# A cross network's first layer: weights in three transfers, first products by input tile

## The chip, the cores and the metric

The kernel runs on one core of one Trainium2 chip. The metric is the device time of one execution in microseconds (us), of which the median over several runs is taken. A core has TensorE (PE in the profile, with PEld for its weight loads), VectorE (DVE), ScalarE (ACT), GpSimd (POOL), SyncE (SP, which issues nearly all DMAs here) and 16 DMA engines.

## The reference

Six layers of a cross network over 16384 rows of 416 features, in bfloat16:

```python
B, F, D, L = 16384, 26, 16, 6
Din = min(F * D, 1024)                      # 416
def reference(x0, ws, bs):
    x = x0
    for l in range(L):
        proj = jnp.einsum('bd,de->be', x, ws[l]) + bs[l]
        x = x0 * proj + x
    return x
```

## The kernel before

The rows are cut into 8 groups of 2048 (`GC`), a group into 4 chunks of 512 (`CH`, index `j`). On the chip x stands transposed: features on the partitions, rows along the free axis. The 416 features are three tiles of 128 (`NT` = 3, index `t` as input, `i` as output) and a tail of 32. A product is one matmul of a 128 x 128 piece of `wm[l]` with a 128 x 512 chunk of x into one of 8 PSUM banks; three products and a tail matmul (`w3[l]`, `rows32`) make one output tile of one chunk. `evacuate` then adds the bias on ScalarE, and multiplies by x0 and adds x on VectorE.

All instructions are put in order by hand: `add` appends each to the queue of its engine with the tokens it reads and writes, and `Program` works out the semaphore waits between engines. Within an engine the order is that of the calls. A token for PSUM is a whole bank, `("ps", b)`: a reader of a bank waits for the last writer of it that stands ahead of it, and a writer for all its earlier readers.

Groups other than the first are loaded by transposing DMAs. Group 0 is loaded in natural order, as rows on partitions, in eight transfers of half a chunk each (`load_nat(j, k0, k1)`, L758), and transposed on TensorE: `transposed_chunk(j)` (L813) makes 12 transposes of 128 x 128 for a chunk, six for its first half and six for its second, then copies the three tiles out of PSUM into `x0s`, on VectorE (L823) or on ScalarE (L825). Where the tiles of chunk j lie in PSUM is fixed by two banks:

```python
ba, bb = ((0, 1), (3, 0), (6, 7), (0, 1))[j]
place = ((ba, 0), (bb, 0), (ba, CH)) if j == 0 else ((ba, 0), (ba, CH), (bb, 0))
```

and a tile is copied by VectorE where `(b == bb) != (j == 1)`. So VectorE copies tile 1 of chunk 0, tiles 0 and 1 of chunk 1 and tile 2 of chunks 2 and 3, and ScalarE the others: two of chunk 0, one of chunk 1, two of chunk 2, two of chunk 3.

`first_job` is the start of the kernel: the transposes of chunk 0, those of the bias, fill matmuls on constants (`keep_busy(n, b)`, n pieces of 128 columns, L795), the products of chunk 0 for output tiles 0 and 1 (`full`, L668), the transposes of chunks 1 and 2, the products of chunk 1, the transposes of chunk 3 and the tails (`transposed_tails`, L833), and then the products of chunks 2 and 3 with their tail matmuls (L689), output tile by output tile. The products of chunk j go to banks `ba[j]` and `bb[j]` with `ba, bb = [4, 5, 6, 7], [2, 3, 0, 1]`.

Layer 0's weights are loaded in two transfers (`load_wm(0, "sp", f0, f1)`, L392): columns 0 to 255 (output tiles 0 and 1) behind chunk 0's rows, the others behind the tail weights (`load_w3`, L401). Then `load_group(1)` issues the transposing DMAs of group 1 (L411, L421). After the first job come two tiles of group 1 (`two_tiles`) and, for nearly all of the time, a stream of matmuls on 32-row strips whose order is a string in the code (`ORDER`, L1108 and L1112).

Of the kernel before, what the change touches and what calls it, by code (L numbers as in the profile page):

```python
# [3 lines left out]
P = 128  # L4
# [302 lines left out]
def bass_standalone__cross_network_dcn__recsys_kernel(  # L307
# [6 lines left out]
    B, D = x0.shape  # L314
# [61 lines left out]
    def bank(b, p0=0, p1=P, n=CH):  # L376
        return psum[p0:p1, b * CH:b * CH + n]
# [7 lines left out]

    W0 = 2 * P

    def load_wm(l, eng, f0=0, f1=D):  # L390
        toks = {0: [("wm", l)], W0: [("wm", l, "rest")]}[f0] if l == 0 else [("wm", l), ("wm", l, "rest")]
        add(eng, lambda h: h.dma_start(  # L392
            wm[l][:, :, f0:f1], ws[l, 0:NT * P, f0:f1].rearrange("(t p) f -> p t f", p=P)),
            writes=toks, lane=f"wm{l}_{f0}", batch=0)

    def wm_tok(l, i):
        return ("wm", l) if i < 2 else ("wm", l, "rest")

    def load_w3(l, eng):
        for j in range(NJ):  # L400
# [252 lines left out]
    def full(g, l, i, banks, first, chunk_major, after_chunk=None, chunks=range(NJ), ts_=range(NT), columns=False):  # L653
        src, stok = x_src(g, l)
        ecols = slice(i * P, (i + 1) * P)
        seq = [(t, j) for j in chunks for t in ts_] if chunk_major else \
              [(t, j) for t in ts_ for j in chunks]
        for t, j in seq:
            if columns:
                for c in range(NJ):  # L660
                    o = slice(c * T32, (c + 1) * T32)
                    add("pe", lambda h, t=t, j=j, c=c, o=o: h.matmul(  # L662
                        psum[o, banks[j] * CH:(banks[j] + 1) * CH],
                        wm[l][:, t, i * P + c * T32:i * P + (c + 1) * T32], src(t, j, j + 1),
                        start=(first and t == 0), stop=(not first and t == NT - 1), tile_position=(0, c * T32)),
                        reads=[stok(t, j), wm_tok(l, i)], writes=[("ps", banks[j])])
                continue
            add("pe", lambda h, t=t, j=j: h.matmul(  # L668
                bank(banks[j]), wm[l][:, t, ecols], src(t, j, j + 1),
                start=(first and t == 0), stop=(not first and t == NT - 1)),  # L670
                reads=[stok(t, j), wm_tok(l, i)], writes=[("ps", banks[j])])
            if after_chunk and t == NT - 1:
                after_chunk(j)

# [20 lines left out]
    def tails(batch, corners_last=False, banks=None):  # L695
# [14 lines left out]
        for (g, l), b in zip(batch, bs_):  # L710
            src, stok = x_src(g, l)
            for t in range(NT):
                for j in range(NJ):
                    ro, qo = quad(g, l + 1, j)
                    add("pe", lambda h, t=t, j=j, src=src, l=l, b=b, ro=ro, qo=qo: h.matmul(  # L715
                        psum[qo, b * CH:(b + 1) * CH], wm[l][:, t, NT * P:D], src(t, j, j + 1),
                        start=(corners_last and t == 0), stop=(not corners_last and t == NT - 1),
                        tile_position=(0, ro * T32)),
                        reads=[stok(t, j), wm_tok(l, NT)], writes=[("ps", b)])
            if not corners_last:  # L720
                evacuate_tail(g, l, b)
        if corners_last:
# [41 lines left out]
        reads=["warm"], writes=["warm"])  # L764
    load_nat(0, 0, 2)
    load_nat(0, 2, KK)
    load_wm(0, "sp", 0, W0)
    for j in range(1, NJ):
        load_nat(j, 0, 2)
        load_nat(j, 2, KK)  # L770
    load_w3(0, "sp")
    load_wm(0, "sp", W0, D)
    load_group(1)

    def second_tails():
# [51 lines left out]
    def transposed_tails(b):  # L827

        s = slot(0)
        for k in range(KK):  # L830
# [6 lines left out]
        add("dve", lambda h: h.tensor_copy(x0s[s][:, XW:XW + CH], psum_t(b)[:, 0:CH]),  # L837
            reads=[("ps", b)], writes=x03_toks(s))

    def first_job():  # L840

        g, l = 0, 0
# [7 lines left out]
        for j in range(NJ):  # L850
# [17 lines left out]
        transposed_tails(7)  # L868
        full(g, l, 0, ba, True, True, chunks=[2, 3])
# [194 lines left out]
    def stream(run):  # L1064
# [23 lines left out]
        for _, r, c, b in plan:  # L1088
# [18 lines left out]
            if t < NT:  # L1107
                add("pe", lambda h, l=l, t=t, j=j, b=b, q=q, ecols=ecols, src=src, kw=kw: h.matmul(  # L1108
                    bank(b), wm[l][q, t, ecols], src(t, j, j + 1)[q, :], **kw),
                    reads=[stok(t, j), wm_tok(l, i)], writes=[("ps", b)], row=r)  # L1110
# [60 lines left out]
    def nat_full(kk, j, b, first, ts=range(NT)):  # L1171
        for t in ts:
            add("pe", lambda h, t=t: h.matmul(  # L1173
                bank(b, n=D), xcol(t, j, kk), wm[l][:, t, :], start=(first and t == 0),
                stop=(not first and t == NT - 1)),
                reads=[stok(t, j), ("wm", l)], writes=[("ps", b)])

    def turn_last(j, b):

# [139 lines left out]
```

## Time and profile before

| | |
|---|---|
| median of 3 runs | 465.24 us (465.17 to 465.78) |
| the profiled execution | 465.03 us |
| its span, from the first to the last instruction | 463.2 us |
| TensorE busy | 458.1 us, 99% of the span |
| VectorE, ScalarE busy | 402.9 us, 87%; 382.2 us, 83% |
| fill matmuls before the first products | 4.90 to 5.35 us |
| first products (L668) start | 5.55 us |
| first tail matmul (L689) of the first output tile | 12.21 us |

The view by line gives busy time and the wait ahead of a group; the timeline gives start and length of each piece of work, merged where instructions of one kind follow each other, with the idle time ahead of it and what ended it in brackets. In the chain the times of a matmul are those of its end as modelled, some 0.15 us later than the starts in the timeline; times in the text are starts by the timeline. A start is counted from the span's start.

### The profile page before, as it was taken

The numbers are of one execution on the slowest core, as the hardware profiler recorded it, in microseconds if no ns is written. First come the engines' busy times: TensorE is split into PE (matmuls) and PEld (weight loads), VectorE is DVE, ScalarE is ACT, GpSimd is POOL, SyncE is SP. The second block draws the span as 40 slices with busy tenths as digits, with TensorE's granted clock in tenths as the row PEclk, the third lists the DMA queues.
The fourth block names the chain that finished last, engine by engine and source line by source line (L and its number), as shares of the span: only waits on it lengthen the run. The fifth ranks groups of instructions, "written<-read, shape, count | busy, mean of one in ns | idle before, by whom it ended". The sixth has DMA issues, their size and how long they took to land.

```text
span 463.2 us, 17830 instructions
## 1 busy us (share of the span) xinstructions
PE 458.1 (99%) x8001; PEld 266.1 (57%) x8001; DVE 402.9 (87%) x697; ACT 382.2 (83%) x609; POOL 10.7 (2%) x15
## 2 busy tenths in 40 slices
PE   9999999999999999999999999999999999999996
PEld 5444656575655556555665556566556565555552
DVE  2897898988889898898989889898988988989997
ACT  4686889887988889797888889888888888888785
POOL 1000000000000000000000000000000040000000
PEclk9999999999999999999999999999999999999999
DMA  8986759000002859086477965690000088171899
GB/s 229 188 178 148 153 110 195 14 23 10 17 4 37 145 178 192 15 131 182 89 130 137 196 104 94 104 226 17 25 2 4 25 143 299 41 132 43 213 163 307
DMA packets 136768, 53.78 MB, mean 116 GB/s; under 512 B 113258, under 2 KB 135284, under 8 KB 136692
## 3 DMA queue, kind: packets, MB, share of 16 engines
q1 hardware_dynamic: 136536, 52.54, 53.2%
q8 instruction: 62, 1.02, 0.9%
q10 hardware_dynamic: 156, 0.11, 0.1%
q14 instruction: 14, 0.11, 0.1%
HBM read 5.97 MB, written 13.63 MB: 42 GB/s over the span
## 4 chain that ended last, share of the span: by engine, by line
PE 94%; DVE 4%; DMA 1%; issue 0%; SPq 0%; ACT 0%; DVEq 0%
PE ps L1108 73%; PE ps L715 7%; PE ps L1112 6%; PE ps L668 4%; PE ps L662 1%; PE ps L703 1%; DVE x L1234 1%; DVE x L591 1%; DVE x L1228 1%; DMA wm<-in_ws_dram 1%; DVE tw L586 1%; PE ps L689 1%; PE ps L813 0%; SPq L758 0%; ACT tw L574 0%
## 5 line engine op out<-in xcount | busy, mean ns | idle before, releaser
L1108 PE MATMUL ps<-x,wm 32*128 32x512 bf16 x6288 | 372.8, 374 | 0.0
L574 ACT ACTIVATE tw<-ps,bias 128x512 bf16<-128x512 f32 x524 | 327.2, 688 | 48.5 <-PE ps L1108 35.8
L1108 PEld LDWEIGHTS ps<-x,wm 32*128 32x128 bf16 x6288 | 221.9, 92 | 135.5 <-ACT tw L574 6.5
L586 DVE TENSOR_TENSOR tw<-tw,x 128x1024 bf16<-128x1024 bf16 x262 | 177.2, 690 | 41.5 <-ACT tw L574 40.1
L591 DVE TENSOR_TENSOR x<-tw,x 128x1024 bf16<-128x1024 bf16 x262 | 170.5, 686 | 0.3
L1112 PE MATMUL ps<-x,w 32*128 32x512 bf16 x524 | 159.5, 374 | 0.0
L1112 PEld LDWEIGHTS ps<-x,w 32*128 32x128 bf16 x524 | 44.6, 92 | 6.0
L715 PE MATMUL ps<-x,wm 128*32 128x512 bf16 x564 | 33.6, 380 | 0.0
L635 ACT ACTIVATE ts<-ps,bias 128x512 bf16<-128x512 f32 x32 | 20.4, 686 | 13.1 <-PE ps L703 13.1
L538 ACT ACTIVATE tw<-ps,bias 128x1024 bf16<-128x1024 f32 (+1 forms) x24 | 20.7, 938 | 8.1 <-PE ps L689 7.0
L715 PEld LDWEIGHTS ps<-x,wm 128*32 128x32 bf16 x564 | 13.5, 96 | 18.2 <-ACT tw L574 3.7
L668 PE MATMUL ps<-x,wm 128*128 128x512 bf16 x92 | 21.3, 380 | 0.2 <-DMA wm<-in_ws_dram 0.2
L639 DVE TENSOR_TENSOR x<-ts,x 128x512 bf16<-128x512 bf16 x47 | 18.4, 420 | 0.3
L951 POOL COPY ost<-ot 128x512 bf16<-128x512 bf16 x6 | 9.2, 1534 | 389.8 <-DMA ot<-x 389.8
L547 DVE TENSOR_TENSOR tw<-tw,x 128x1024 bf16<-128x1024 bf16 (+1 forms) x21 | 13.1, 637 | 2.2 <-ACT tw L538 2.1
L668 PEld LDWEIGHTS ps<-x,wm 128*128 128x128 bf16 x92 | 8.4, 98 | 11.4 <-issue 2.1
L631 DVE SCALAR_TENSOR_TENSOR ts<-ps,bias,x 128x512 bf16<-128x512 f32 x15 | 11.2, 747 | 3.1 <-PE ps L703 3.1
L552 DVE TENSOR_TENSOR x<-tw,x 128x1024 bf16<-128x1024 bf16 (+1 forms) x21 | 12.6, 634 | 0.0
L637 DVE TENSOR_TENSOR ts<-ts,x 128x512 bf16<-128x512 bf16 x32 | 12.4, 418 | 0.0
L1173 PE MATMUL ps<-wm,x 128*128 128x416 bf16 x48 | 9.3, 340 | 0.0
L823 DVE COPY x<-ps 128x512 bf16<-128x512 bf16 x5 | 2.0, 423 | 8.1 <-PE ps L813 8.1
L1222 ACT ACTIVATE x<-ps 128x416 bf16<-128x416 f32 x16 | 7.7, 528 | 1.5 <-PE ps L1173 1.5
(51 smaller groups left out, 72.0 us busy)
## 6 DMA issues: line engine op xcount, KB each, us to landing
out_dram<-ost SPq DMA_DIRECT2D x6, 1664.0 KB, 8.3
x<-x SPq DMA_DIRECT2D x24, 96.0 KB, 2.2
x<-in_x_dram SPq DMA_DIRECT2D x8, 208.0 KB, 3.6
x<-in_x_dram SPq DMA_DIRECT2D x4, 416.0 KB, 8.0
wm<-in_ws_dram SPq DMA_DIRECT2D x5, 312.0 KB, 3.5
x<-x SPq DMA_DIRECT2D x22, 64.0 KB, 2.4
out_dram<-x SPq DMA_DIRECT2D x3, 416.0 KB, 3.2
out_dram<-ost SPq DMA_DIRECT2D x2, 416.0 KB, 3.1
```

What stands on the lines that cost most here:

```text
L538: add("act", lambda h, a=a, w=w, b0=b0: h.activation(tw[r][:, a * CH:(a + w) * CH], psum[:, b0 * CH:(b0 + w) * CH], ACT_F.Identity, bias=b ...
L547: add("dve", lambda h, a=a, e=e: h.tensor_tensor(tw[r][:, a * CH:e * CH], tw[r][:, a * CH:e * CH], x0s[s0][:, i * GC + a * CH:i * GC + e * ...
L552: add("dve", lambda h, a=a, e=e: h.tensor_tensor(xs[so][:, i * GC + a * CH:i * GC + e * CH], tw[r][:, a * CH:e * CH], src(i, a, e), ALU.ad ...
L574: add("act", lambda h: h.activation(tw[r][:, j * CH:(j + 1) * CH], bank(b), ACT_F.Identity, bias=bias[:, i, l:l + 1], scale=1.0), reads=[( ...
L586: add("dve", lambda h: h.tensor_tensor(tw[r][:, o], tw[r][:, o], x0s[s0][:, c], ALU.mult), reads=[("tw", r, k) for k in both] + [x0_tok(s0 ...
L591: add("dve", lambda h: h.tensor_tensor(xs[so][:, c], tw[r][:, o], src(i, a, a + 2), ALU.add), reads=[("tw", r, k) for k in both] + [stok(i ...
L635: add("act", lambda h: h.activation(ts[r][:, :], bank(b), ACT_F.Identity, bias=bias[:, 3, l:l + 1], scale=1.0), reads=[("ps", b), "bias"], ...
L639: add("dve", lambda h: h.tensor_tensor(x3s[so][:, :], ts[r][:, :], res, ALU.add), reads=[("ts", r)] + rtok, writes=[("x3", so), ("x3", so, ...
L668: add("pe", lambda h, t=t, j=j: h.matmul(bank(banks[j]), wm[l][:, t, ecols], src(t, j, j + 1), start=(first and t == 0), stop=(not first a ...
L715: add("pe", lambda h, t=t, j=j, src=src, l=l, b=b, ro=ro, qo=qo: h.matmul(psum[qo, b * CH:(b + 1) * CH], wm[l][:, t, NT * P:D], src(t, j, ...
L1108: add("pe", lambda h, l=l, t=t, j=j, b=b, q=q, ecols=ecols, src=src, kw=kw: h.matmul(bank(b), wm[l][q, t, ecols], src(t, j, j + 1)[q, :], ...
L1112: add("pe", lambda h, l=l, b=b, q=q, ecols=ecols, s3=s3, kw=kw: h.matmul(bank(b), w3[l][q, ecols], s3[q, :], **kw), reads=tok3 + [("w3", l ...
```

## The change

The first layer's weights come in three transfers of 104 KB, one for each input tile, all columns of it, in the order 1, 0, 2; there is no second transfer behind the tail weights. Each product of layer 0 waits for its own input tile only. The products of chunks 0 and 1 go by input tile: for each input tile both output tiles, in the order 1, 0, 2 for chunk 0 and 0, 2, 1 for chunk 1 (`by_copy`). The transposes of each half chunk follow the same order (1, 0, 2 for chunks 0, 2 and 3). `transposed_chunk` may make one half only: chunk 2's first half stands ahead of chunk 1's products, its second half with its copies behind them. The fill matmuls ahead of the first products shrink from 5 pieces of 128 columns to 2.

```diff
-    W0 = 2 * P
-    def load_wm(l, eng, f0=0, f1=D):
-        toks = {0: [("wm", l)], W0: [("wm", l, "rest")]}[f0] if l == 0 else [("wm", l), ("wm", l, "rest")]
+    def load_wm(l, eng):
         add(eng, lambda h: h.dma_start(
-            wm[l][:, :, f0:f1], ws[l, 0:NT * P, f0:f1].rearrange("(t p) f -> p t f", p=P)),
-            writes=toks, lane=f"wm{l}_{f0}", batch=0)
+            wm[l][:, :, :], ws[l, 0:NT * P, :].rearrange("(t p) f -> p t f", p=P)),
+            writes=[("wm", l, t) for t in range(NT)], lane=f"wm{l}", batch=0)
+    def load_wm_tile(l, t):
+        add("sp", lambda h: h.dma_start(wm[l][:, t, :], ws[l, t * P:(t + 1) * P, :]),
+            writes=[("wm", l, t)], lane=f"wm{l}_{t}", batch=0)
...
     load_nat(0, 0, 2)
     load_nat(0, 2, KK)
-    load_wm(0, "sp", 0, W0)
+    for t in (1, 0, 2):
+        load_wm_tile(0, t)
     for j in range(1, NJ):
         load_nat(j, 0, 2)
         load_nat(j, 2, KK)
     load_w3(0, "sp")
-    load_wm(0, "sp", W0, D)
     load_group(1)
...
-    def transposed_chunk(j):
+    def transposed_chunk(j, halves=(0, 2)):
...
-        for k2 in (0, 2):
-            for t in range(NT):
+        for k2 in halves:
+            for t in by_copy(j):
...
+        if 2 not in halves:
+            return
         for t in range(NT):
             b, o = place[t]
...
+    def by_copy(j):
+        return (0, 2, 1) if j == 1 else (1, 0, 2)
+
+    def by_input_tile(j, *bks):
+        src, stok = x_src(0, 0)
+        for n, t in enumerate(by_copy(j)):
+            for i, b in enumerate(bks):
+                add("pe", lambda h, n=n, t=t, i=i, b=b: h.matmul(
+                    bank(b[j]), wm[0][:, t, i * P:(i + 1) * P], src(t, j, j + 1),
+                    start=n == 0, stop=False), reads=[stok(t, j), ("wm", 0, t)], writes=[("ps", b[j])])
...
-        keep_busy(5, 3)
+        keep_busy(2, 3)
         ba, bb = [4, 5, 6, 7], [2, 3, 0, 1]
-        full(g, l, 0, ba, True, True, chunks=[0])
-        full(g, l, 1, bb, True, True, chunks=[0])
+        by_input_tile(0, ba, bb)
         transposed_chunk(1)
-        transposed_chunk(2)
-        full(g, l, 0, ba, True, True, chunks=[1])
-        full(g, l, 1, bb, True, True, chunks=[1])
+        transposed_chunk(2, (0,))
+        by_input_tile(1, ba, bb)
+        transposed_chunk(2, (2,))
         transposed_chunk(3)
         transposed_tails(7)
```

In the other places of the diff a product's token of the weights becomes `("wm", l, t)`.

More of the change, by code (lines that the diff above doesn't have):

```diff
@@ L384, in take @@
         return got
-    W0 = 2 * P
-    def load_wm(l, eng, f0=0, f1=D):
-        toks = {0: [("wm", l)], W0: [("wm", l, "rest")]}[f0] if l == 0 else [("wm", l), ("wm", l, "rest")]
+    def load_wm(l, eng):
         add(eng, lambda h: h.dma_start(
-            wm[l][:, :, f0:f1], ws[l, 0:NT * P, f0:f1].rearrange("(t p) f -> p t f", p=P)),
-            writes=toks, lane=f"wm{l}_{f0}", batch=0)
-    def wm_tok(l, i):
-        return ("wm", l) if i < 2 else ("wm", l, "rest")
+            wm[l][:, :, :], ws[l, 0:NT * P, :].rearrange("(t p) f -> p t f", p=P)),
[3 more added lines that the diff above has]
+            writes=[("wm", l, t)], lane=f"wm{l}_{t}", batch=0)
     def load_w3(l, eng):
@@ L665, in full @@
                         start=(first and t == 0), stop=(not first and t == NT - 1), tile_position=(0, c * T32)),
-                        reads=[stok(t, j), wm_tok(l, i)], writes=[("ps", banks[j])])
+                        reads=[stok(t, j), ("wm", l, t)], writes=[("ps", banks[j])])
                 continue
@@ L670, in full @@
                 start=(first and t == 0), stop=(not first and t == NT - 1)),
-                reads=[stok(t, j), wm_tok(l, i)], writes=[("ps", banks[j])])
+                reads=[stok(t, j), ("wm", l, t)], writes=[("ps", banks[j])])
             if after_chunk and t == NT - 1:
@@ L718, in tails @@
                         tile_position=(0, ro * T32)),
-                        reads=[stok(t, j), wm_tok(l, NT)], writes=[("ps", b)])
+                        reads=[stok(t, j), ("wm", l, t)], writes=[("ps", b)])
             if not corners_last:
@@ L1109, in stream @@
                     bank(b), wm[l][q, t, ecols], src(t, j, j + 1)[q, :], **kw),
-                    reads=[stok(t, j), wm_tok(l, i)], writes=[("ps", b)], row=r)
+                    reads=[stok(t, j), ("wm", l, t)], writes=[("ps", b)], row=r)
             else:
@@ L1175, in nat_full @@
                 stop=(not first and t == NT - 1)),
-                reads=[stok(t, j), ("wm", l)], writes=[("ps", b)])
+                reads=[stok(t, j), ("wm", l, t)], writes=[("ps", b)])
     def turn_last(j, b):
```

## The prediction

> **What bounds the kernel now.** I read the page first: TensorE (PE) is 99% busy, and the chain that ended last lies on it.
>
> ```profile
> PE 94%; DVE 4%; DMA 1%; issue 0%; SPq 0%; ACT 0%; DVEq 0%
> ```
>
> So a shift of TensorE's stream in the first 12 us, which is all that this change touches, reaches the end one for one: no later row shows a wait that could swallow it or add to it. Next the chain in order of time over the first 24 us (start, length, what):
>
> ```profile
> 1.65 3.76 DMA wm<-in_ws_dram
> 5.42 0.14 issue
> 5.55 1.46 PE ps L668 x6
> 7.00 1.00 PE ps L813 x18
> 8.01 0.03 issue
> 8.04 0.51 PE ps L813 x6
> 8.55 1.29 PE ps L668 x6
> 9.84 0.67 PE ps L813 x12
> 10.51 0.34 PE ps L833 x16
> 10.85 1.43 PE ps L668 x6
> ```
>
> The first products (L668) wait for the weight transfer, issued at 1.65, landed at 5.42. From there TensorE runs 24 transposes (chunks 1 and 2, L813), six products of chunk 1, 12 transposes of chunk 3, the tails (L833), and the products of chunks 2 and 3. The one hole is at 8.01, where the second half of chunk 2's rows has only just landed (7.99). Third, the timeline of the same stretch, for the copies out of PSUM:
>
> ```profile
> 4.62 0.42 DVE L823 COPY x<-ps 128x512 bf16<-128x512 bf16 x1 [3.75 <-PE ps L813]
> 4.74 1.08 ACT L825 ACTIVATE x<-ps 128x512 bf16<-128x512 bf16 x2 [1.90 <-PE ps L813]
> ...
> 7.60 0.76 DVE L823 COPY x<-ps 128x512 bf16<-128x512 bf16 x2 [2.55 <-PE ps L813]
> 7.71 0.60 ACT L825 ACTIVATE x<-ps 128x512 bf16<-128x512 bf16 x1 [1.81 <-PE ps L813]
> 8.47 1.09 ACT L825 ACTIVATE x<-ps 128x512 bf16<-128x512 bf16 x2 [0.17 <-PE ps L813]
> ...
> 10.44 1.08 ACT L825 ACTIVATE x<-ps 128x512 bf16<-128x512 bf16 x2 [0.88 <-PE ps L813]
> 10.55 0.42 DVE L823 COPY x<-ps 128x512 bf16<-128x512 bf16 x1 [1.54 <-PE ps L813]
> ```
>
> ScalarE takes 0.60 us for one copy and 1.09 for two, so each further one adds 0.49. It copies two tiles of chunk 2 (8.47 to 9.56) and two of chunk 3 (10.44 to 11.52); between them it has 0.88 us to spare, and the product that needs its last copy begins at 11.69, 0.17 after it. Last, the DMA queue. The chunk halves (208 KB, L758) are issued 0.43 to 0.48 apart; narrow windows of the DMA view give their landings: chunk 0 at 3.24 and 4.07, chunk 1 at 5.99 and 6.53, chunk 2 at 7.39 and 7.99, chunk 3 at 8.69 and 9.36. Ahead of the weights the queue runs thin (0.42 is the share of the DMA engines):
>
> ```profile
> 3.25:3.75 0.50, 0.50 (x6) 0.46 (x5) 0.00 (x0) 0.00 (x0) 0.00 (x0) 1.00 0.42 112
> ```
>
> **The change, part by part.** Before, product 5 of the six that end this stage (chunk 3, tile 1 of the input) starts at 11.69; I work out where it stands after. Steps on TensorE: a transpose each 0.056 us (12 in 0.67), a product each 0.216 us (six in 1.29).
>
> *Weights in three.* SP issues three transfers of 104 KB where it had one of 192 KB (0.88 us) and, behind the rows, one of 120 KB (0.43). At 0.43 each the three take 1.29, so the rows of chunks 1 to 3 and the tail weights are issued 0.41 later, and the transposing loads of group 1 at the old time (-0.02). The tail weights are needed at 12.21 and landed at 10.69; the second weight transfer landed at 10.95 for a use at 14.49, so its removal is worth nothing and the later issue costs nothing there. For the rows I need their shift d in landing. The old transfer landed 1.35 after chunk 0's second half. The halves land 0.54 to 0.86 apart, mostly near 0.67. If a tile costs by its bytes (half of 0.54), three take 0.81, d = -0.54, which the later issue limits to -0.51 (2.98 + 2.5, the shortest time to landing, against 5.99); if it costs like a half, 0.67, three take 2.0 and d = +0.66. I take d = -0.1, nearer to the bytes, because the thin half microsecond above (0.58 of 0.5 us, 0.29, unused) can be filled once the first tile needs a third of the pieces.
>
> A rule of the Trainium skill speaks against this: DMA: Bandwidth & Descriptors, section Bandwidth, asks for large batches and calls small transfers dominated by descriptors, with 0.95 us for 64 KB and 6.15 for 1 MB. By it a tile would be near 1.2 us (an estimate by its table), three 3.6, and d would be +2.2. The row above, 208 KB each 0.67 with several in flight, speaks for overlap instead.
>
> *First products by input tile.* The order (1, 0, 2) puts tile 1's transposes first. Its bank is whole two transposes earlier (0.11 us), so VectorE's copy goes from 4.62 to 4.51 and ends at 4.94; ScalarE's two stay at 4.74, as both its tiles share a bank that is finished last, and end at 5.33 and 5.82. The fill matmuls shrink from 640 columns to 256 (0.16 us at a product's pace); they lay in the wait for the weights, and end now near 5.01, so they cost nothing either way. With this d the tiles land 0.42 apart from 4.07 on, at 4.5, 4.9 and 5.3, and are never last (at 0.67 apart the third is, by 0.2). Two products start at 5.02, two at 5.45, two when ScalarE's second copy is in, 5.90; the six end at 6.33 against 6.84. Gain here: 0.51 us, if each extra wait on two semaphores adds nothing.
>
> *Chunk 1 and half of chunk 2.* Twelve transposes from 6.33 (rows in by 5.9 and 6.43): the last starts at 6.95. The new order (0, 2, 1) ends with the bank that VectorE copies twice, so VectorE starts at 6.95 + 0.26 = 7.21 and ends at 7.96 (0.76). Chunk 2's first half lands at 7.29, is done at 7.67. Product 1 could go then, but product 2 (tile 0 of the input, second output tile) writes bank 3, out of which VectorE is still copying: it waits for the second copy, 8.05 with the release. Before, six more transposes covered that wait. Product 1 and product 2 being adjacent in the queue, all transposes and products behind them wait too. The six end at T = 8.05 + 5 x 0.216 = 9.13.
>
> *Second half of chunk 2, at T instead of 8.04.* Four transposes complete ScalarE's bank at T + 0.43 = 9.56 (three steps of 0.056, then 0.26 for end and release). Its four copies now stand in one row: 0.60 + 3 x 0.49 = 2.07, ended at 11.63. The product that needs the last goes 0.08 later, at 11.71. TensorE itself would be there at T + 0.34 + 1.10 + 4 products and the bank's release, 0.91, that is 11.48: it now waits 0.23 for ScalarE.
>
> **Sum.** 11.71 against 11.69: +0.02 us. The 0.51 gained at the first products is lost in VectorE's second copy and in ScalarE's row, which loses the 0.88 of slack it had. The profiled execution took 465.03 us (span 463.2 and 1.83 around it), 0.21 under the median of the three runs; 465.05 then stands for a median of 465.26. Such a difference is under what a measurement can tell here: about 0.2%, 0.93 us, and the three runs alone lie 0.61 apart.
>
> **Rivals.** *The gain stays.* If chunk 2's rows land 0.4 earlier (the bound by bytes allows 0.51) and VectorE's second copy is out of the way sooner than its row says, T is TensorE's own work, 6.33 + 18 transposes (1.01) + 1.29 = 8.63; with ScalarE's row behind it, 8.63 + 2.58 = 11.21, it is -0.48: 464.8. For it speaks that TensorE is the chain; against it that two copies of known length would have to be hidden.
>
> *The rows come late.* The three tiles stand ahead of chunk 1's rows. The place is the wait for the first half of chunk 2: T is the larger of 9.13 and 9.07 + d, so it decides from d = 0.06, and each microsecond beyond is one lost. At the bound d = +0.66 it is +0.62: 465.9. The estimate by the skill's table (d = +2.2, DMA: Bandwidth & Descriptors) would make it 467.4. Against it stands the thin queue at 3.25.
>
> *The clock falls back.* The first six transposes of chunk 0 take 0.85 us, the next six 0.50: until about 4.1 TensorE works at half pace (though the granted-clock column has 1.00 there), and that is 3.4 us after its first fill matmul at 0.77. The change takes fill away and leaves holes of about 0.25 (for chunk 2's rows) and 0.1 to 0.2 (for the copies). If they cost the full pace once, for a stretch like the opening's, 1.7 us are lost: 467.0, slower beyond doubt. It decides from how much idling is let pass; the old stream had holes of 0.2 and 0.15 without harm, and TensorE was busy for 3.30 of the 3.50 us from 4.10. TensorE: Matmul & The Clock Gate in the Trainium skill (Part 1: The HAM clock gate) says half pace comes after an idle window of about 3.4 us; by that rule holes of a quarter are harmless, and this trace agrees as far as it goes.
>
> *Nothing happens at all* is out: the first products cannot start where they did once tile 1 and its copy are in.
>
> **How the numbers follow.** Forecast, within 0.2 us of before: 0.68. Gain stays, down to -0.48: 0.13. Rows late: 0.10, of which 0.02 beyond +0.93. Clock: 0.03. Something later in the stream that no row shows, 0.03 to either side beyond 0.2%. So faster 0.03, same 0.68 + 0.13 + 0.08 = 0.89, slower 0.02 + 0.03 + 0.03 = 0.08. The range goes from the kept gain, with 0.2 for the spread of runs, 464.6, to the late rows' bound, 465.9.
>
> **What would show it.** After: first products near 5.0, ended near 6.3; TensorE's second product of chunk 1 waiting for VectorE (L823); ScalarE's four copies back to back from about 9.6 to 11.6; the fifth product behind them waiting on ScalarE; the tail weights' matmuls at 12.2 as before. Wrong if ScalarE's copies are not adjacent, if chunk 2's rows are waited for longer than 0.3, or if the first stage ends as forecast and the total still moves by a microsecond.

## The result, and the profile after

| | before | after |
|---|---|---|
| median of 9 runs each | 465.37 us (465.17 to 466.19) | 466.56 us (465.90 to 467.21) |
| ratio, 95% interval | | 1.0024 [1.0015, 1.0032] |
| the profiled execution (its span) | 465.03 us (463.2) | 466.39 us (464.6) |
| first products of chunk 0 start | 5.55 us | 4.69 us |
| first half of chunk 2 landed | 7.39 us | 8.21 us |
| first tail matmul | 12.21 us | 12.97 us |
| last product | 458.72 us | 459.52 us |

The changed kernel is 1.2 us slower by the medians, 0.70 to 1.49 by the interval; 465.3 was forecast, and 465.9 was the upper end of the range. The prediction was wrong. Three executions of this study, one of them of the kernel before, ran for 803 to 1236 us in a slow state and are left out of all medians.

The share of the chain by engine, from the page of the changed kernel:

```profile
PE 93%; DVE 4%; DMA 1%; SPq 1%; issue 0%; ACT 0%; DVEq 0%
```

One thing is new: SyncE's queue (SPq) has a percent, and the view of the chain in order of time shows where (start, length, what):

```profile
1.65 0.43 SPq L394
2.08 0.04 issue
2.12 0.43 SPq L394
...
2.59 0.43 SPq L394
...
3.07 0.43 SPq L756
...
3.54 0.43 SPq L756
...
4.01 4.19 DMA x<-in_x_dram
...
8.25 0.51 PE ps L811 x6
8.76 1.29 PE ps L847 x6
...
10.32 1.09 ACT x L825 x2
...
11.46 1.58 PE ps L666 x6
```

Both chains begin with the issues of chunk 0's two halves (to 1.61). Before, the weight transfer followed (1.65 to 5.42), and from there the chain lay on TensorE. Now three issues for the weight tiles follow (L394), then two for the halves of chunk 1 (L756), then the transfer of the first half of chunk 2, 4.19 us from its issue to its landing, and the chain comes to TensorE at 8.25. Behind that stands ScalarE's row of copies. TensorE in the timeline (start, length, what, the wait ahead and its releaser), one row of the kernel before and then the changed kernel:

```profile
6.84 1.71 PE L813 MATMUL ps<-ident,x 128*128 128x128 bf16 x24
```

```profile
4.69 1.46 PE L847 MATMUL ps<-x,wm 128*128 128x512 bf16 x6
6.63 1.14 PE L811 MATMUL ps<-ident,x 128*128 128x128 bf16 x12 [0.48 <-DMA x<-in_x_dram]
8.25 0.51 PE L811 MATMUL ps<-ident,x 128*128 128x128 bf16 x6 [0.48 <-DMA x<-in_x_dram]
...
9.89 1.17 PE L811 MATMUL ps<-ident,x 128*128 128x128 bf16 x18
...
12.97 0.40 PE L687 MATMUL ps<-x,w 32*128 32x512 bf16 x4
```

The first products run 0.86 us earlier than before, with no wait for weights. Then TensorE waits for rows twice, 0.48 us each time, where before its 24 transposes of chunks 1 and 2 stood in one row, with a hole of 0.2 at most: the gain of the start is spent at a place that stood behind the weights before and now stands in the open. The copies, in the same view:

```profile
7.81 0.76 DVE L823 COPY x<-ps 128x512 bf16<-128x512 bf16 x2 [3.20 <-PE ps L811]
10.32 2.06 ACT L825 ACTIVATE x<-ps 128x512 bf16<-128x512 bf16 x4 [2.02 <-PE ps L811]
```

ScalarE's four copies stand back to back, as forecast. From the first tail matmul on the two traces run in parallel: the changed kernel is 0.76 us late at 12.21, 0.77 late at 300 us and 0.80 late at the last product. The other 0.56 us between the two profiled executions lies behind the last product, where the last stores land (4.50 us before, 5.06 after); it goes from 4.4 to 5.1 over all profiles of this study whatever the kernel, 4.47 in a second profile of the changed one. The stretch from the first tail matmul to the last product goes from 446.1 to 447.0, so a start can be read into an end to a few tenths only.

### The profile page after: what moved, and what is told of

Same layout as the page of the kernel before. It is cut to its first block, busy times and chain, and to the rows that moved or that the text cites. A ratio compares the mean times of both kernels' runs of the same rounds, so it can differ in the third digit from the quotient of the medians.

```text
span 464.6 us, 17831 instructions
## 1 busy us (share of the span) xinstructions
PE 457.9 (99%) x8000; PEld 266.6 (57%) x8000; DVE 403.0 (87%) x697; ACT 381.8 (82%) x609; POOL 7.0 (2%) x15
## 4 chain that ended last, share of the span: by engine, by line
PE 93%; DVE 4%; DMA 1%; SPq 1%; issue 0%; ACT 0%; DVEq 0%
PE ps L1118 73%; PE ps L713 7%; PE ps L1122 6%; PE ps L666 4%; PE ps L660 1%; PE ps L701 1%; DVE x L1244 1%; DMA x<-in_x_dram 1%; DVE x L589 1%; DVE x L1238 1%; DVE tw L584 1%; PE ps L687 1%; SPq L756 0%; SPq L394 0%; PE ps L847 0%
## 5 line engine op out<-in xcount | busy, mean ns | idle before, releaser
L666 PE MATMUL ps<-x,wm 128*128 128x512 bf16 x80 | 18.4, 380 | 0.1
L666 PEld LDWEIGHTS ps<-x,wm 128*128 128x128 bf16 x80 | 7.2, 97 | 10.2 <-issue 1.8
L961 POOL COPY ost<-ot 128x512 bf16<-128x512 bf16 x6 | 5.6, 928 | 391.0 <-DMA ot<-x 391.0
```

What stands on the lines that cost most here:

```text
L666: add("pe", lambda h, t=t, j=j: h.matmul(bank(banks[j]), wm[l][:, t, ecols], src(t, j, j + 1), start=(first and t == 0), stop=(not first a ...
```

## The experiments

The chip's time is told as the median, the difference to the kernel before run beside it, and the ratio with its interval. The intervals reach some 0.4 us to either side, and more where a kernel had four runs, so differences of a few tenths are read only where the profile says the same. Starts and landings are those of one profiled execution of each kernel; the same landing differs by 0.92 us between the two profiles of the changed kernel. In the cuts of code, `...` and lines of comment stand for what is left out.

### The change in its two halves

`order_alone` keeps the changed order and loads the weights as the kernel before does.

```diff
-    for t in (1, 0, 2):
-        load_wm_tile(0, t)
+    load_cols(0, 2 * P, ...)          # 192 KB, as before
...
     load_w3(0, "sp")
+    load_cols(2 * P, D, ...)          # 120 KB, as before
```

> The new order of transposes, products and fill, with the two weight transfers of before. If the three weight transfers are the whole cause (theory A), the rows land as before (chunk 2's first half near 7.4) and the time is that of before, within 0.2 us. If the order has a price of its own (theory B, the two copy waits of the prediction's working): the first six products run from 5.55 to 6.84 as before, the last transpose of chunk 1 starts at 7.46, VectorE's second copy ends 1.01 later, the products of chunk 1 end at 7.46 + 2.18 = 9.64, and the first tail matmul stands at 12.7 instead of 12.21: +0.5 us.

Measured: 465.99 us, +0.37; 1.0007 [0.9997, 1.0017]. TensorE's timeline:

```profile
8.19 1.58 PE L855 MATMUL ps<-x,wm 128*128 128x512 bf16 x6 [0.18 <-DVE x L831]
9.61 1.17 PE L819 MATMUL ps<-ident,x 128*128 128x128 bf16 x18
```

Here the wait is the forecast one, for VectorE's second copy, and the rows come in time (first half of chunk 2 at 6.94). The six products end at 9.61; the prediction's formula, with the last transpose of chunk 1 at 7.45 as in this profile, gives 9.63. So the profile shows a price of the order, some 0.4 us; by the runs alone it is not shown, as the interval still holds no change.

`loads_alone` keeps the order before and takes the three transfers (in the order 0, 1, 2).

```diff
-    load_wm(0, "sp", 0, W0)
+    for t in range(NT):
+        load_wm_tile(0, t)
...
-    load_wm(0, "sp", W0, D)
```

> The three weight transfers (in the order 0, 1, 2) with the order of transposes, products and fill of before. If the transfers push the rows of chunks 1 to 3 back as the changed kernel's profile has it (chunk 2's second half landed at 9.18, 1.19 later), the old order, which needs that half ahead of chunk 1's products, loses all of it: first tail matmul near 13.4, +1.2 us, as much as the whole change. If the late rows of that profile were one execution's chance, chunk 2's second half lands near 8.0 and the time is that of before.

Measured: 466.16 us, +0.54; 1.0010 [1.0001, 1.0020]. The chain, in order of time:

```profile
4.85 4.16 DMA x<-in_x_dram
```

The second half of chunk 2, at 7.99 before, lands at 9.00, and the first tail matmul stands at 13.22, 1.0 later; by the medians the loss is about half of that. The two halves of the change come to 0.37 + 0.54 = 0.91, and the whole change measured 1.19 in the first comparison and, run again, 0.86. That they add up is not to be read as two prices side by side: in the changed order the products of chunk 1 end by the later of two waits (copies or rows), not by their sum.

`after_again` is that second run of the changed kernel, in another batch.

> The changed kernel once more, beside the others on one chip. In every profile so far the time from the first tail matmul to the last product was 446.5 us, and 4.4 to 5.1 us came after that. If the loss lies in the start alone, the first tail matmul stands near 13.0 again and the time is +0.8 to +1.2 us over before. If the first profile's late rows were mostly one execution's stalls, the first tail matmul is near 12.3 here.

Measured: 466.51 us, +0.86; 1.0016 [1.0007, 1.0024]. Its profile has the rows later still: the first half of chunk 2 was issued at 4.18 and landed at 9.12, and the first tail matmul stood at 13.89. In both profiles it starts 4.77 us behind that landing (8.21 to 12.97, 9.12 to 13.89).

### Which part of the order costs

`chunk0_tiles` is the kernel before, in which chunk 0 alone goes by input tile, with the short fill.

```diff
-            for t in range(NT):
+            for t in ((1, 0, 2) if j == 0 else range(NT)):
...
-        keep_busy(5, 3)
+        keep_busy(2, 3)
-        full(g, l, 0, ba, True, True, chunks=[0])
-        full(g, l, 1, bb, True, True, chunks=[0])
+        # chunk 0's six products, input tiles 1, 0, 2, both output tiles each
```

> The kernel of before with chunk 0 alone in the new order (transposes and products by input tile, shorter fill); weights, chunks 1 to 3 as before. If the order's price of 0.4 us lies in the products of chunk 1 between the two halves of chunk 2 (VectorE's second copy, ScalarE's four copies in a row), this kernel shows none of it: within 0.2 us of before. If it lies in the shorter fill or in chunk 0's order, it is +0.4 us.

Measured: 465.31 us, -0.07; 1.0001 [0.9993, 1.0010]. This part shows no cost and no gain, so the order's price, as far as there is one, lies in the rest of it: the products of chunk 1 between the two halves of chunk 2, where `order_alone` shows them waiting for VectorE's second copy.

### What makes the rows late

`one_load` has the changed order and one transfer of all 312 KB.

```diff
-    for t in (1, 0, 2):
-        load_wm_tile(0, t)
+    load_cols(0, D, ...)
```

> The new order, with all of the first layer's weights in one transfer of 312 KB (384 pieces of 832 bytes, as in the three). If bytes or pieces push the rows back, chunk 2's first half lands near 8.2 as with three transfers; if it is the number of transfers and their issue, near 7.4 to 7.6. The first products wait for all weights, near 5.7 to 5.9 instead of 4.7. The time is near that of the changed kernel either way (+1.0 us over before, between +0.6 and +1.3).

Measured: 466.70 us, +1.08; 1.0028 [1.0016, 1.0041]. The one transfer lands at 6.45, so chunk 0's products wait 1.18 us for it. It loses as much as the three tiles, at another place. The first half of chunk 2 lands at 8.09; in `order_alone`, with 120 KB less ahead of rows that are issued at the same time (2.45), it landed at 6.94. So more bytes ahead do make the rows late, but here TensorE does not wait for them. Three of the ten runs took 467.9 to 468.2 us; why is not known, but `bytes_only` below is a like case.

`tiles_64k` has the changed order and three transfers of 64 KB (columns 0 to 255 of each tile), the other 120 KB behind the tail weights.

```diff
-        add("sp", lambda h: h.dma_start(wm[l][:, t, :], ws[l, t * P:(t + 1) * P, :]),
+        add("sp", lambda h: h.dma_start(wm[l][:, t, 0:2 * P], ws[l, t * P:(t + 1) * P, 0:2 * P]),
```

> The new order with three transfers by input tile of columns 0 to 255 alone (64 KB each, 384 pieces of 512 bytes) and the other columns behind the tail weights as before. If the bytes push the rows back (120 KB fewer stand ahead of them here), chunk 2's first half lands near 7.5 and the time is +0.1 us over before; if the pieces or the issue of three transfers do it, it lands near 8.2 as with 104 KB and the time is +0.8 us.

Measured: 466.05 us, +0.43; 1.0009 [0.9999, 1.0018]. That is the price of the order (+0.37) and hardly more, although the rows are issued as late as in the changed kernel (3.08). The first half of chunk 2 lands at 8.01, near the 8.2 that was to mean that the bytes are not the cause; the time lies between the two forecasts. The first tail matmul is at 12.78, again 4.77 behind that landing, and only 0.09 behind `order_alone`, which the copies hold up as long. About half a microsecond is left up to the changed kernel's +0.86 and +1.19. The 120 KB ahead of the rows may be its cause; the landings (8.01 against 8.21 and 9.12) agree, but they scatter too widely to show it.

`tiles_twice` is the changed kernel with three more transfers of 104 KB (another layer's weights) ahead of the rows.

```diff
     for t in (1, 0, 2):
         load_wm_tile(0, t)
+    for t in range(NT):
+        add("sp", lambda h, t=t: h.dma_start(wm[5][:, t, :], ws[5, t * P:(t + 1) * P, :]), ...)
```

> The changed kernel with three more transfers of the same kind and size (another layer's weights, which are loaded again later) right behind its three, ahead of the rows. If the transfers ahead of the rows are what costs, at the pace of the profile's pieces (0.53 us for a tile) the rows land 1.6 us later again, chunk 2's first half near 9.8, first tail matmul near 14.5, and the time is +1.6 us over the changed kernel. If the start's loss lies in the order of products and copies, the added transfers fill idle time in part and the time is at most +0.5 us over it.

Measured: 468.12 us, +2.47 over before and 1.61 over the changed kernel; 1.0053 [1.0036, 1.0069]. The late rows are on the path and grow with what stands ahead: the first half of chunk 2 lands at 9.53. Part of it is not theirs: the profiled execution fell to half the clock for a stretch (last section).

`rows_whole` is the changed kernel with the rows of chunks 1 to 3 in three transfers of 416 KB, to see whether fewer, longer transfers flow better.

```diff
-        load_nat(j, 0, 2)
-        load_nat(j, 2, KK)
+        load_nat(j, 0, KK)
```

> The changed kernel with the rows of chunks 1 to 3 in three transfers of 416 KB (128 pieces of 3328 bytes) instead of six of 208 KB. If the stalls of single DMA engines come with the number of pieces and of transfers being issued, the queue is quicker: all of chunk 2 lands by 8.3 (its two halves landed at 8.2 and 9.2, 9.1 and 9.8 in the two profiles of the changed kernel), and the time is 0.4 us over before at most. If the bytes set the pace, it lands at 9.2 to 9.8 as before, its first transposes wait for all of it, and the time is +1.5 us or more over before.

Measured: 467.88 us, +2.5; 1.0061 [1.0046, 1.0076]. Whole chunks land at 7.80, 9.15 and 10.29; in the changed kernel's first profile the second halves do so at 7.22, 9.18 and 10.43, in its second at 7.93, 9.79 and 10.93. Fewer transfers move them no faster than the first and somewhat faster than the second, and nothing can start on half a chunk. That the number of row transfers slows the queue is not borne out.

### Another queue

`before_act` is the kernel before, with its 192 KB issued by ScalarE's queue.

```diff
+    load_wm(0, "act", 0, W0)
     add("act", lambda h: h.dma_start(brow[0:L, :], bs[:, :]), ...)
...
-    load_wm(0, "sp", 0, W0)
```

> The kernel of before, with its one transfer of 192 KB issued by ScalarE's queue behind the biases instead of SyncE's. The rows of chunks 1 to 3 are issued 0.9 us earlier. If the rows' issue and the thin half microsecond at 3.25 cost time there, chunk 2's second half lands near 7.6, the hole of 0.2 us ahead of its transposes goes, the first products start at 5.4 on ScalarE's copy, and the time is -0.3 us. If rows and weights only share the engines, the weights land after 5.6, the first products start later by as much, and the time is 0 to +0.3 us.

Measured: 465.54 us, -0.11; 0.9991 [0.9982, 0.9999], at most a small gain. The same bytes move. The rows of chunk 1 are issued at 1.65 in place of 2.57, and the two halves of chunk 2 land at 6.20 and 6.77, 1.2 us earlier than in the profile before. That time has no use in the old order: VectorE's copies of chunk 1 (ended at 8.67) stand ahead of the products there.

`act_tiles` does the same to the changed kernel.

```diff
-        add("sp", lambda h: h.dma_start(wm[l][:, t, :], ...
+        add("act", lambda h: h.dma_start(wm[l][:, t, :], ...
```

> The changed kernel with the three weight transfers issued by ScalarE's queue, behind the biases; SyncE issues the rows of chunks 1 to 3 right behind those of chunk 0, 1.4 us earlier than in the changed kernel. If it is the later issue that makes the rows late, chunk 2's first half lands at 7.2 or before and the time is within 0.2 us of before or better. If it is the weights' bytes and pieces on the same 16 DMA engines, it lands near 8 again and the time is that of the changed kernel (+1.0 us).

Measured: 466.68 us, +1.03; 1.0021 [1.0012, 1.0030]. TensorE's timeline:

```profile
6.64 0.59 PE L847 MATMUL ps<-x,wm 128*128 128x512 bf16 x2 [0.63 <-DMA wm<-in_ws_dram]
7.50 0.59 PE L847 MATMUL ps<-x,wm 128*128 128x512 bf16 x2 [0.27 <-DMA wm<-in_ws_dram]
```

The rows of chunk 2 come earlier (7.60), but now stand ahead of two of the tiles, which land at 6.50 and 7.37. The lateness is moved, not removed.

`chunk0_act` puts the chunk 0 part and ScalarE's queue together on the kernel before (the edits of `chunk0_tiles` and `before_act`).

> The same, with the transfer of 192 KB issued by ScalarE's queue as in the run of that name. The first products then wait for VectorE's copy of tile 1 alone and start 0.3 us earlier than there, the rows are in early enough for all transposes of chunks 1 and 2 to follow at once, and nothing else changes: 0.3 us less than that kernel, 0.4 to 0.6 us less than before. If the copies out of PSUM or the clock of the first 5 us set the start instead, it is level with that kernel (-0.1 to -0.4 us against before).

Measured: 465.06 us, -0.32; 0.9991 [0.9982, 1.0000]. It is the lowest median of this study, but the interval reaches 1.0000, so a gain is not shown.

### Bytes, issue, or number

`before_again` is one more execution of the kernel before, for a second profile of it.

> The kernel of before once more, for a second profile of its start. From the medians (465.6 less 1.8 around the span, 446.5 of stream and about 4.5 of tail) the first tail matmul should stand near 12.8 in an ordinary execution, later than the 12.21 of its first profile, because TensorE reaches its full pace later or rows land later; if 12.21 was ordinary, it stands there again and the changed kernel's loss must lie partly behind the start.

Measured: 465.18 us, first tail matmul at 12.34. The 12.21 of the first profile was ordinary. But the issue of the 192 KB took SyncE 0.49 us there and not 0.88:

```profile
1.65 0.49 SPq L392 DMA_DIRECT2D wm<-in_ws_dram  x1
```

So the rows were issued at 2.18: measured against that, the changed kernel issues them 0.9 later and not 0.5. Issued 0.39 earlier than in the first profile, the rows of chunk 2 landed no earlier (7.43 and 7.98 against 7.39 and 7.99).

`issue_only` is the kernel before with two transfers of 2 KB between the weights and the rows.

```diff
     load_wm(0, "sp", 0, W0)
+    for k in (0, 1):
+        add("sp", lambda h, k=k: h.dma_start(w3[5][k * 32:k * 32 + 16, 0:64], ...), ...)
```

> The kernel of before with two transfers of 2 KB between the weights' transfer and the rows of chunk 1: no bytes to speak of, but 0.95 us more of issue ahead of those rows (0.47 each). If rows land a fixed time after they are issued, chunk 2's second half lands near 8.9 instead of 8.0, the first tail matmul stands near 13.1 and the time is +0.7 to +0.9 us. If the DMA engines' pace sets the landing and the issue is only a floor (the step of the prediction), the landing moves by at most 0.3 and the time stays within 0.2 us of before.

Measured: 466.30 us, +0.60; 1.0017 [1.0008, 1.0026]. Four kilobytes and 0.95 us of SyncE cost about as much as the three tiles of `loads_alone`. The profile doesn't show where: it is of the fastest of the eleven runs (465.80), and in it the halves of chunk 2 land only 0.12 and 0.25 later than before (7.51, 8.24), with the first tail matmul at 12.46. On the landing the forecast of a shift of at most 0.3 held; the time is nearer to the other one.

`bytes_only` is the kernel before with all 312 KB in its one transfer, none behind the rows.

```diff
-    load_wm(0, "sp", 0, W0)
+    # one transfer, columns 0 to 415
...
-    load_wm(0, "sp", W0, D)
```

> The kernel of before with the whole of the first layer's weights, 312 KB, in its one transfer, and none behind the tail weights: 120 KB more ahead of the rows of chunk 1, issued no later than before. If bytes at the rows' pace (208 KB in 0.6 us) are the price, rows and weights land 0.35 us later, and the time is +0.2 to +0.5 us. If the issue alone makes the rows late, they land as before and only the weights land later: 0 to +0.2 us.

Measured: 466.39 us, +0.69; 1.0019 [1.0008, 1.0030]. Eight runs lie from 465.74 to 466.70 (median 466.12, +0.42), three at 467.75 to 468.16; the profiled one is of the three, and half clock (last section) takes part of its time. The halves of chunk 2 land 0.74 later than before (8.13, 8.73), though their rows are issued 0.44 earlier. But the weights land late too (6.47), and chunk 0's products wait 1.05 us for them. So bytes alone make rows late and cost something; what the late rows alone cost is not told by this run.

One question was left. Over the profiles the engines moved 348 to 380 GB/s from 5.25 to 8.25 us where the rows were issued between 2.13 and 2.57, and 270 to 321 where three or more transfers stood ahead of them on SyncE's queue, in `issue_only` too. That could be the number of transfers or the lateness of the issue. `wait_only` is the kernel before, in which the first rows of chunk 1 wait for ScalarE's first activation and nothing is added ahead of them.

```diff
         add("sp", lambda h: h.dma_start(x0n[:, j, k0:k1, :], perm(g0, j)[:, k0:k1, :]),
+            reads=["warm"] if (j, k0) == (1, 0) else [],
```

> The kernel before, with its weight transfers, in which the first transfer of chunk 1's rows also waits for ScalarE's first activation, which ended at 2.85 us in the kernel with the two small transfers; the rows are then issued from about 2.95, and nothing more is transferred or issued ahead of them. In the profiles so far the DMA engines moved 348 to 397 GB/s from 5.25 to 8.25 us where no more than one transfer stood on SyncE's queue between chunk 0 and chunk 1, and 270 to 320 where three stood there. Theory A (the number of transfers ahead makes those behind slower): the rate stays above 340, the rows come later only by part of the 0.4 to 0.8 us, and the time is within 0.3 us of before. Theory B (a later issue is enough, whatever causes it): the rate in that stretch falls to about 300 and the time rises by 0.6 us as with the two small transfers.

Measured: 465.98 us, +0.55; 1.0012 [1.0003, 1.0021]. Its chain, in order of time, begins on ScalarE, waits for the second half of chunk 2 and then comes to TensorE:

```profile
2.63 0.22 ACT warm L764
...
2.86 0.34 SPq L758
...
4.19 4.33 DMA x<-in_x_dram
```

The halves of chunk 2 land at 7.90 and 8.53, half a microsecond later than before, while those of chunk 1 land as before (5.94, 6.66); the first tail matmul stands at 12.75. `tiny_act` adds the two small transfers on ScalarE's queue, so that the rows are not delayed.

```diff
+    for k in (0, 1):
+        add("act", lambda h, k=k: h.dma_start(w3[5][k * 32:k * 32 + 16, 0:64], ...), ...)
```

> The kernel before, with two more transfers of 2 KB at the start, issued by ScalarE's queue, so that the rows of chunk 1 are issued as early as before (2.2 to 2.6 us) but as many transfers stand ahead as in the kernel that issued them on SyncE's queue. Theory A (the number of transfers ahead makes those behind slower, whatever queue issues them): 270 to 320 GB/s from 5.25 to 8.25 us and 0.6 us more than before. Theory B (it is the issue on SyncE's queue, which delays what stands behind it): 350 GB/s or more and the time of before, within 0.2 us.

Measured: 465.40 us, -0.03; 0.9999 [0.9990, 1.0008]. The same stretch in the view by windows (us, busy time of PE, PEld, DVE, ACT and POOL with instructions, granted clock, share of the DMA engines, GB/s), of the kernel before, the changed kernel, `wait_only` and `tiny_act` in this order:

```profile
5.25:8.25 3.00, 2.77 (x30) 1.82 (x29) 0.65 (x2) 1.19 (x4) 0.24 (x1) 1.00 1.01 356
```

```profile
5.25:8.25 3.00, 1.92 (x17) 0.79 (x15) 0.44 (x2) 0.88 (x3) 0.00 (x0) 1.00 0.93 301
```

```profile
5.25:8.25 3.00, 2.79 (x26) 1.49 (x24) 0.55 (x2) 1.28 (x4) 0.44 (x1) 1.00 0.96 334
```

```profile
5.25:8.25 3.00, 2.70 (x26) 1.60 (x24) 0.39 (x2) 1.09 (x4) 0.40 (x1) 1.00 1.00 364
```

| rows of chunk 1 first issued at | GB/s from 5.25 to 8.25 | first half of chunk 2 landed | kernels |
|---|---|---|---|
| 2.13 to 2.57 us | 348 to 380 | 6.94 to 8.13 us | before (two profiles), `order_alone`, `one_load`, `chunk0_tiles`, `bytes_only`, `tiny_act` |
| 2.86 us | 334 | 7.90 us | `wait_only` |
| 3.07 to 3.42 us | 274 to 321 | 7.51 to 9.12 us | after (two profiles), `loads_alone`, `tiles_64k`, `rows_whole` (whole chunk at 9.15), `issue_only` |
| 4.68 us | 270 | 9.53 us | `tiles_twice` |

`act_tiles`, with its rows issued from 1.65 on, has 369; in `before_act` and `chunk0_act` the last rows land at 8.06 and 8.44, so the stretch says little of them.

What is shown is the time: a later issue alone costs some 0.6 us in the old order (`issue_only`, and `wait_only` with an issue 0.3 to 0.7 late), with intervals clear of no change, and the same two transfers cost nothing where the rows are issued on time (`tiny_act`). So the number of transfers is not the cause, as far as two small ones can tell. How the later issue costs is not shown. The rate goes with the time of issue, and `wait_only`'s 334 lies between what the two theories had; the landings go with it only loosely. `tiny_act`, issued on time, has the first half of chunk 2 at 7.79 and the first tail matmul at 12.58, both later than in `issue_only`'s profile. Why the engines move less in that stretch stays open.

## Why the prediction was wrong

**The step that failed** is the term d, the shift of the rows' landing. It was put at -0.1, with +0.66 as its upper bound; the two profiles have +0.82 and +1.73. The three tiles themselves were sized well: they landed at 4.26, 4.93 and 5.24, so the last came 0.18 before the old transfer's 5.42. Three things were wrong in the working. First, d was taken as the tiles' shift, as if the rows followed at the old distance. They do not: the first half of chunk 1 landed 0.57 behind the old transfer, and 1.35 and 1.46 behind the third tile in the two profiles. The later issue was used as a limit on a gain only, not as a cost, and `wait_only` and `issue_only` show that it is one. It is not the whole of that distance: `issue_only` issues the same rows at 3.12 and has them at 5.79, the changed kernel at 3.07 and has them at 6.59. Second, the 0.41 us of later issue is too short. It leaves out the 0.04 between issues (the halves start 0.46 to 0.53 apart; 0.43 to 0.48 is how long an issue takes), and the measured delay is 0.50. And it was read off one profile, in which the old weight transfer took SyncE 0.88 us; in five other profiles of the kernel before and its variants the same issue took 0.43 to 0.49 (0.76 in `order_alone`), and against those the delay is 0.9. Third, the thin half microsecond was filled, but with little. The window at 3.25 of the changed kernel:

```profile
3.25:3.75 0.50, 0.50 (x8) 0.46 (x7) 0.00 (x0) 0.00 (x0) 0.00 (x0) 1.00 0.68 225
```

225 GB/s in place of 112 are 56 KB more. Of the 120 KB that were pulled ahead of the rows, more than half remain, and the three us behind 5.25 then moved 301 GB/s in place of 356, which is 165 KB less. Together some 230 KB, at 301 GB/s 0.8 us, is what d was in this profile; the same estimate gives 1.2 for the second, which had 1.73, so it is not the whole account.

**The size of it.** In the changed order a late row is partly harmless, as T is the larger of 9.13 and 9.07 + d. In `order_alone` the rows (6.94, d = -0.45) would allow 8.62 and the copies set 9.61, so it has 1.0 to give; in `tiles_64k` the rows land 1.07 later and the first tail matmul stands 0.09 later. In the changed kernel they land later again, by 0.20 and 1.11, and the first tail matmul moves by 0.20 and 1.11. With d = 0.82 the formula gives all of the first profile's loss at the first tail matmul (0.78 forecast by it, 0.76 measured), with nothing left for the order; where the first products start as late as before, the copies alone would cost 0.4 to 0.5 and the rows the rest. How the late rows divide into issue and bytes is not settled: in the old order a later issue cost 0.55 to 0.60, and both together 0.54 (`loads_alone`), so they do not add.

**Right, and shown.** The shift passes to the end one for one (0.76 at 12.21, 0.80 at the last product). T is 9.07 + d: with d = 0.82, 9.89, and the timeline has 9.89. ScalarE's row was forecast at T + 0.43 to T + 2.50 and stands at 10.32 to 12.38, that is T + 0.43 to T + 2.49. The product behind it was forecast at T + 2.58 and starts at 12.44, T + 2.55. Where the rows are in time, VectorE's second copy is the wait (`order_alone`). Not foreseen was that the first product of chunk 2 also waits for ScalarE, at 11.46 (both tiles of that copy's bank must be out); the later copy hides it.

**The order.** It was forecast at +0.02 as a balance: 0.51 gained at the first products against what VectorE's second copy and ScalarE's row take back. Without the gain the same working gives 0.51 more, +0.53, and `order_alone` comes near it: its weights land at 5.32, its six first products end when they did before, and its first tail matmul is at 12.69 against 12.21, +0.48 (+0.37 by the medians). In the changed kernel the gain is there or not with the pace of TensorE (last section): the first products start at 4.69 in one profile and at 5.49 in the other, against 5.55 before.

**The rivals.** "The rows come late" is what happened, with its place and its formula; its price was bounded too low, and its chance, 0.10, with it. One of the prediction's own signs of being wrong, a wait of more than 0.3 for chunk 2's rows, came: 0.48. The estimate from the table of DMA: Bandwidth & Descriptors in the Trainium skill (section Bandwidth) had put d at +2.2. That table is for transfers issued from GpSimd, and these are SyncE's: the tiles do not land that far apart (0.67 and 0.31), yet d in the second profile is nearer to it than to the value taken. "The clock falls back" did not happen in the changed kernel's profiles, in which the granted clock is 1.00 throughout the start. "The gain stays" would have needed rows 0.4 early.

## What to carry to other kernels

A transfer that others queue behind can cost them its issue (some 0.6 us here), and not only its bytes: before splitting one, count how much later everything behind it on that queue is issued, and consider another engine's queue for it. Time gained at the front of a stream is kept only if each later input comes earlier too, so follow it up to the first wait that does not move. A duration that a forecast hangs on (here 0.88 us for an issue, 4.1 us for the start of full pace) should be looked up in several executions, or the range should hold what a second one could show.

## What the runs showed of the hardware

**The start of full pace moves from run to run.** TensorE works at half pace at first, and the prediction put the change of pace at 4.1 us, from one profile. Over the profiles it lies between 3.4 and 6.7 us, worked out from the lengths of the transposes and products. The first six transposes take 0.53 us in the changed kernel's first profile. In its second, and then chunk 0's products in `chunk0_act` and in the changed kernel's second profile:

```profile
3.39 0.84 PE L811 MATMUL ps<-ident,x 128*128 128x128 bf16 x6
...
5.49 1.73 PE L847 MATMUL ps<-x,wm 128*128 128x512 bf16 x6
```

```profile
5.50 2.01 PE L864 MATMUL ps<-x,wm 128*128 128x512 bf16 x6
```

The six products take 1.46 us where the pace is full. An earlier start of these products is thus paid back in part by slow products: in `chunk0_act` the weights were there at 4.53, and the products still ended later than in the kernel before. TensorE: Matmul & The Clock Gate in the Trainium skill (Part 1) says that the window of this gate runs freely and puts the spread at ±500 ns; that it varies agrees, but here the spread is about 3 us.

**The clock can fall although TensorE is partly busy.** In `tiles_twice` the granted clock was halved from 10.45 to 13.86, behind a stretch of the same length in which TensorE waited 2.02 us for rows; in `bytes_only` from 6.91 to 10.33, behind one with a wait of 1.05 us for the weights. By windows (clock third from the end), first `tiles_twice`, then `bytes_only`:

```profile
7.03:10.45 3.42, 1.55 (x19) 1.14 (x21) 0.76 (x2) 0.60 (x1) 0.00 (x0) 1.00 0.93 315
10.45:13.86 3.41, 3.41 (x18) 2.02 (x19) 0.42 (x1) 0.66 (x2) 0.00 (x0) 0.50 1.08 191
```

```profile
3.50:6.91 3.41, 2.02 (x25) 1.23 (x24) 0.42 (x1) 1.17 (x3) 0.45 (x1) 1.00 0.98 286
6.91:10.33 3.42, 3.42 (x20) 2.09 (x19) 0.16 (x1) 0.00 (x0) 0.00 (x0) 0.50 1.03 253
```

TensorE was busy for 45% and 59% of the stretch ahead. It was busy for 65% of the like stretch in `one_load` (2.23 of 3.41 us from 4.59) and for 68% in the changed kernel's second profile (2.31 from 6.03), and there the clock stayed. The stretches are counted in steps of 3.41 us from the change of pace in each profile. Half pace for 3.41 us costs about 1.7 us, the price that the prediction gave this rival. TensorE: Matmul & The Clock Gate in the Trainium skill (Part 1) asks for an idle window of about 3.4 us; the length agrees, but these two windows were about half busy. Four profiles don't make a threshold, and no run sought it.
